# Block products in one more token group, with the forms of w4 on VectorE

## The chip, the cores and the metric

One core of one Trainium2 chip runs the kernel. The metric is the device time of one execution in microseconds (us). PE is the matrix engine, DVE the vector engine, ACT the scalar engine, POOL the GpSimd engine, SP the engine whose queue issues the DMAs.

## The reference

With x of 2048 tokens by 448 channels, `_layernorm` without gain and the tanh form of gelu:

```python
def _A_ref(x, w_r, w_i):              # spectral filter
    X = rfft2(x, axes=(-2, -1))
    X = X * (w_r + 1j * w_i)
    return irfft2(X, s=(S, D), axes=(-2, -1))
def _B_ref(x, w1, w2, w3, w4):        # shifted token mixing, then an MLP of width 1792
    h = _gelu(_layernorm(x) @ w1)
    hs = shifted(h) @ w2              # four quarters of the channels, tokens shifted by +1, -1, +2, -2
    x1 = x + hs
    h2 = _gelu(_layernorm(x1) @ w3) @ w4
    return x1 + h2
xn = _layernorm(x)
return x + _A_ref(xn, A_w_r, A_w_i) + _B_ref(xn, B_w1, B_w2, B_w3, B_w4)
```

All inputs and the output are fp32.

## The kernel before

fp32 operands are split into two fp16 numbers, a high and a low half (`hi`, `lo`), and a product is made as hi x hi + hi x lo + lo x hi, three passes on PE.

**The MLP.** The 2048 tokens are eight groups G of 256 (two blocks of 128), the 1792 hidden channels seven pairs fp of 2 x 128. One unit (G, fp) is a `front` and a `back`. `front` multiplies w3 by the tokens (22 matmuls of 256 columns into one PSUM bank), then ACT applies gelu and writes the high half of h (`hf`, L776), and DVE writes the low half (L777). `back` multiplies h by w4 into the two accumulators `acc` of the group, over all seven fp: 12 matmuls of 448 columns for two token blocks, two channel tiles and three passes.

In the groups named in `STR` (5, 6 and 7 before), the two cross passes hi x lo and lo x hi, 8 of the 12 matmuls, are made another way (`crossed`): the 2 x 2 blocks (token block by channel tile, channel tile by column half) are multiplied with seven products in place of eight, as in Strassen's scheme. Each product is a matmul of 224 columns for either pass, 14 in all; hi x hi stays as 4 matmuls of 448 columns. This needs sums and differences ("forms") of h, made by `forms` on DVE into `hgm` (three operations per unit, L786 to L788), forms of w4, made once by `w4_forms` into `w4x` (its lines L928 to L932), and two more PSUM accumulators `cr` from the banks with the tag "tr". At the end of such a group, `back` copies `cr` out by ACT into `cross` (L843), makes four additions there (L846), evacuates `acc` by DVE (L835), and adds `cross` to the result (L850). `cross` is the memory of `x2mem` from fp32 element 4F on, where w4's raw rows 12 and 13 lay before, and where later the second buffer of the spectral chunks (`pf_buf[1]`) lies.

`steps` writes out the order of the units: the front of unit n+2 goes ahead of the back of unit n (`ahead=AH`), the forms of unit n+1 too. `run` emits them with a late priority (`FILL`); evacuations and forms have the first (`EVAC`). `tags` names the PSUM banks of the fronts: two "mm" banks, or "mm" and "tr" in turn, four banks.

**The spectral part** runs between the units. Folds: for each pair of token blocks, `do_fold` loads x into one of four fold buffers, normalizes it on ACT and adds and subtracts mirrored columns on POOL; `step1_in` splits it (L594 on ACT, L595 on DVE) into `xh`; `step1` multiplies (L604) and splits the result (L608, L609). Then 16 chunks (`chunk_a`, `chunk_b`, `chunk_z`, `chunk_c`) in groups 3 and 4, then 16 inverse steps. `w_scale` loads the filter in eight pieces and takes their maxima on DVE (L269), `w_scale_end` makes a power of two from them with a transpose (L627) and a broadcast (L631) on PE. `ln2` normalizes token blocks for the MLP (L549, L551 on DVE).

**What sets the order.** The program builder orders instructions by priority and a model of their times, and the order is then fixed for each engine. `behind(key)` holds an instruction until the one filed under the key is issued: ("f", G, fp) is the end of a front's evacuation, ("m", G, fp) the last matmul of a back, ("X", b) the load of a fold, ("fold", b) its last addition. The lists `FOLD` (when a fold starts), `PACE` (after which back its matmuls come), `WMAX` (when each maximum is taken) and `LATE` (the normalization of blocks 12 to 15) hold such keys.

Of the kernel before, what the change touches and what calls it, by code (L numbers as in the profile page):

```python
# [12 lines left out]
F32 = mybir.dt.float32  # L13
F16 = mybir.dt.float16
# [17 lines left out]
AH = 2  # L32
PACE = [(0, 6), (1, 1), (1, 2), (1, 4), (1, 5), (2, 0), (2, 1), (2, 3)]
FOLD = [(0, 5), (1, 0), (1, 1), (1, 3), (1, 4), (1, 6), (2, 0), (2, 2)]
PIN = [("a3",), ("a3",), ("a3",), ("a3",)]
WMAX = [(1, 4), (1, 5), (2, 0), (2, 0), (2, 1), (2, 2), (2, 3), (2, 4)]
LATE = [(2, 2), (2, 3), (2, 4), (2, 5)]
HS = 3
STR = (5, 6, 7)
INV, LAG = 4, 2  # L40
EVAC, FILL = 0, 100000

# [80 lines left out]
def body(tc, nc, x, wf, w1, w2, w3, w4, c_g, c_n, c_small, out):  # L123
# [59 lines left out]
    warm = pc.tile([128, 1], F32, name="warm")  # L183
    V.memset(warm, 0.0)
    A.activation(out=warm, in_=warm, func=AF.Gelu_apprx_tanh)
    x2mem = pw.tile([128, 9 * F], F16, name="x2mem")
    wsrc = x2mem[:, 8 * F:8 * F + 512]
    V.memset(wsrc, 0.0)
    ones = pc.tile([128, 128], F32, name="ones")
# [33 lines left out]
    load_w3([2, 3])  # L223
    cross = x2mem.bitcast(F32)[:, 4 * F:4 * F + 2 * D].rearrange("p (i n) -> p i n", i=2)
    x2all = x2mem[:, 0:8 * F].rearrange("p (j t n) -> p j t n", j=4, t=7)
    w4raw = x2mem.bitcast(F32)[:, F:].rearrange("p (f n) -> p f n", f=14)
    W4F = (0, 4, 8, 11, 14)
    w4x = pw.tile([128, 48 * 224], F16, name="w4x")
    hgm = pw.tile([128, 2, 1024], F16, name="hgm")
# [339 lines left out]
    folds = {}  # L569

    def do_fold(b0):
        f = xf_buf[b0 // 2 % 4]
        X = f.rearrange("p b s d -> p (b s d)")[:, 0:2 * D + 2].rearrange("p (b d) -> p b d", b=2)
        after["X", b0] = (SY.dma_start(X[:, :, 0:D], xv[:, b0:b0 + 2]).ins,)
        with behind("f", *FOLD[b0 // 2]):
            for i in range(2):
                x_ = X[:, i, 0:D]
                A.activation(out=x_, in_=x_, func=AF.Identity, scale=xn_scale[b0 + i], bias=xn_bias[b0 + i])
            A.activation(out=X[:, :, D:D + 1], in_=X[:, :, 0:1], func=AF.Copy)  # L579
        ad = X[:, :, 0:D].rearrange("p b (h d) -> p h b d", h=2)[:, :, :, 0:113]  # L580
        bc = X[:, :, 1:D + 1].rearrange("p b (h d) -> p h b d", h=2)[:, ::-1, :, 223:110:-1]
        u = xr.rearrange("p (a b s d) -> p a b s d", a=2, b=2, s=2)
        P.tensor_tensor(out=u[:, 0], in0=ad, in1=bc, op=ALU.add)  # L583
        P.tensor_tensor(out=u[:, 1], in0=ad, in1=bc, op=ALU.subtract)
        for k, op in ((0, ALU.add), (2, ALU.subtract)):
            i = P.tensor_tensor(out=f[:, :, k:k + 2].rearrange("p b s d -> p s b d"), in0=u[:, :, 0], in1=u[:, :, 1], op=op)
        after["fold", b0] = (i.ins,)
        for i in range(2):
            folds[b0 + i] = f[:, i].rearrange("p s d -> p (s d)")
# [201 lines left out]
    def back(G, fp):  # L791
        h = hs.pop((G, fp))
        n = D // 2
        end = 4 if G == 7 else 6
        if fp == 0:
            acc[G] = [bank("acc", f"acc{G}{i}") for i in range(2)]
            if G in STR:
                xs[G] = [bank("tr", f"cr{G}{i}") for i in range(2)]
        if (G, fp) == (7, 5):
            xs[G] = [bank("tr", f"end{i}") for i in range(2)]  # L800
        C = [[(slice(0, D), acc[G][i][:, 0:D], 0, 6)] for i in range(2)]
        if G == 7:
            C[1] = [(slice(0, D), acc[G][1][:, 0:D], 0, 4)]
            if fp > 4:
                C[1] = [(slice(n * k, n * k + n), xs[G][k][:, 0:n], 5, 6) for k in range(2)]
        for i in range(2):
            for r, to, s, e in C[i]:
                with behind("m", G, fp) if (G, fp) == (7, 6) and ("m", G, fp) in after else contextlib.nullcontext():
                    for f in range(2):
                        for hi, wi in ((0, 0),) if crossed(G, fp) else ((0, 0), (0, 1), (1, 0)):  # L810
                            m = T.matmul(to, h[:, hi, 2 * f + i], w4p[0][:, wi, 2 * fp + f, r],  # L811
                                         start=fp == s and f == 0 and hi + wi == 0, stop=fp == e and f == 1 and hi == 1)
                after["m", G, fp] = (m.ins,)
            if not i and not crossed(G, fp):
                yield keep(m)
        if crossed(G, fp):
            g = hg.pop((G, fp))
            X = [xs[G][k // 2][:, n * (k % 2):n * (k % 2) + n] for k in range(4)]
            H = [[acc[G][i][:, n * k:n * k + n] for k in range(2)] for i in range(2)]
            prods = [(0, 1, X[0], 9), (1, 3, H[1][0], 9), (3, 2, H[0][0], C[0][0][3]), (6, 4, X[2], 9),  # L820
                     (4, 5, X[3], end), (5, 6, X[1], end), (2, 7, H[1][1], C[1][0][3])]
            for hi, wi, part in ((0, 1, 0), (1, 0, 0), (0, 1, 1), (1, 0, 1)):
                if hi + part == 1 and wi == part:
                    yield keep(m)
                for k, slot, to, e in prods[3 * part:3 + 4 * part]:
                    m = T.matmul(to, h[:, hi, slot] if slot < 4 else g[:, hi, slot - 4], w4f[fp][k][wi], start=k in (0, 6) and fp == 0 and hi == 0,  # L826
                                 stop=hi == 1 and fp == e)
            after["m", G, fp] = (m.ins,)
        k34 = p34[:, 1:2] if G >= 6 else p34[:, 0:1]
        to = {i: rest[2 * G + i] if G >= 6 else xb(2 * G + i) for i in range(2)} if fp >= 4 else {}  # L830

        def evacuate(i):
            for r, src, _, e in C[i]:
                if fp == e:
                    V.scalar_tensor_tensor(out=to[i][:, r], in0=src, scalar=k34, in1=to[i][:, r], op0=ALU.mult, op1=ALU.add)  # L835
                    if G == 7 and fp == 6:
                        SY.dma_start(ov[:, 2 * G + i, r], to[i][:, r])

        with prio(EVAC):
            if G in STR and fp == end:  # L840
                e0, e1 = cross[:, 0], cross[:, 1]
                for i in range(2):
                    A.activation(out=cross[:, i], in_=xs[G][i][:, 0:D], func=AF.Copy, scale=k34)  # L843
                for o, x, y in ((e0[:, n:], e0[:, 0:n], e0[:, n:]), (e1[:, 0:n], e1[:, 0:n], e0[:, n:]),
                                (e0[:, n:], e0[:, n:], e1[:, n:]), (e1[:, n:], e1[:, 0:n], e1[:, n:])):
                    (V if G == 7 else P).tensor_tensor(out=o, in0=x, in1=y, op=ALU.add)  # L846
            for i in range(2):
                evacuate(i)
                if G in STR and fp == end:
                    (V if G == 7 else P).tensor_tensor(out=to[i], in0=to[i], in1=cross[:, 1 - i], op=ALU.add)  # L850
                if G == 6 and fp == 6:
                    SY.dma_start(ov[:, 2 * G + i], to[i])
        yield keep(m)
# [27 lines left out]
    def mlp(*args, **kw):  # L881
        run(steps(*args, **kw))
# [38 lines left out]
    def w4_forms(fp):  # L921
# [1 line left out]
        b = [[w4p[0][:, :, f + r, n * c:n * c + n] for c in range(2)] for r in range(2)]  # L923
        m = w4all[:, 56 * 224:] if fp == 6 else w4x[:, 8 * 224 * fp:8 * 224 * (fp + 1)]
        m = m.rearrange("p (k n) -> p k n", n=224)
        t1 = [m[:, 6], m[:, 7]]
        t2, t3, t4 = (m[:, k:k + 4:3] for k in range(3))
        P.tensor_tensor(out=t3, in0=b[1][1], in1=b[0][1], op=ALU.add)  # L928
        for i in range(2):
            P.tensor_tensor(out=t1[i], in0=b[0][0][:, i], in1=b[0][1][:, i], op=ALU.subtract)  # L930
            P.tensor_tensor(out=t2[:, i], in0=b[1][1][:, i], in1=t1[i], op=ALU.subtract)
        P.tensor_tensor(out=t4, in0=b[1][0], in1=t2, op=ALU.subtract)  # L932
        w4f[fp] = [[x[:, i] for i in range(2)] for x in (b[0][0], b[1][0], b[1][1], t4)]
        w4f[fp] += [t1] + [[x[:, i] for i in range(2)] for x in (t2, t3)]

    def squares1():
        for t in range(4):
# [165 lines left out]
    Y1 = Y.rearrange("p i q c (b k) -> p i q c b k", k=8)  # L1103
    pfd = pool("pfd", side="right")
    xf_buf = [pfd.tile([128, 2, 4, 113], F32, name=f"xf{i}") for i in range(3)]
    xf_buf.append(hgm.bitcast(F32).rearrange("p i n -> p (i n)")[:, 0:904].rearrange("p (b s d) -> p b s d", b=2, s=4))
    xh_buf = [pfd.tile([128, 2 * 452 + 16], F16, name=f"xh{i}") for i in range(4)]
    for i in range(4):
        P.memset(xh_buf[i][:, 904:], 0.0)
    mlp([1, 2], ahead=AH, tags=("mm", "tr"))  # L1110
    for b in range(0, NB, 2):
        do_fold(b)
        step1_in(b)
        step1_in(b + 1)
        with behind("m", *PACE[b // 2]):
            step1(b)
            step1(b + 1)
    with prio(FILL):
        for fp in range(7):
            with behind("fold", 0 if fp < 2 else 14):  # L1120
                w4_forms(fp)
    ln2(range(12, 16), [A] * 4, LATE)
    with behind("X", 14):
        wm = w_scale()
    close("pfd")
    with behind("m", 2, 5):
        w_scale_end(wm)
    pst = pool("pst", side="right")
    pf_buf = [pst.tile([128, 2, 2, DF], F16, name="pf0"),
# [68 lines left out]
```

## Time and profile before

| | |
|---|---|
| median of 3 runs | 410.64 us (409.51 to 411.13) |
| profiled execution | 409.72 us, its span 407.6 us |
| PE, DVE, ACT, POOL busy | 98%, 75%, 66%, 44% of the span |
| tensor clock granted | 0.999 |

"Busy" is the share of the span in which an engine had an instruction under way. The chain is the sequence of work that ended last, followed back from the last instruction. In listings of groups, the first number behind the bar is busy us, the next the mean ns of one instruction, then idle time before it and what ended it. In a row of waits stand the total in us, the number of times and the longest one. In the timeline and the chain the first number is the start in us from the start of the span, the second the length in us.

### The profile page before, as it was taken

Reading aid. Unit: us, or ns where it says so; the run is one execution under the profiler, and the core shown is the slowest. Engines: PE = TensorE matmul, PEld = TensorE weight load, DVE = VectorE, ACT = ScalarE, POOL = GpSimd, SP = SyncE. Lnnn points to the kernel's source line nnn. Section 1 sums busy time; section 2 is a strip of 40 time slices with the busy share of each in tenths; the row PEclk is TensorE's granted clock in tenths of the full one; section 3 lists DMA queues with packets and bytes.
Section 4 is the critical chain, followed back from the end, with each engine's and each line's share of the span. In section 5 each row is a group of like instructions: output and inputs, shape, how many; then the busy total and the mean of one; then the engine's idle time right before and its main releaser. Section 6 shows DMA issues by size and latency. Waiting matters only on the chain.

```text
span 407.6 us, 8828 instructions
## 1 busy us (share of the span) xinstructions
PE 401.3 (98%) x3379; PEld 296.0 (73%) x3379; DVE 304.2 (75%) x658; ACT 268.6 (66%) x465; POOL 179.8 (44%) x276
## 2 busy tenths in 40 slices
PE   8998999999999999999999999999999999999996
PEld 4553555666767777776888887877788888888885
DVE  5988999899653757894577777763488879889645
ACT  4698993884737865763488888785956566544332
POOL 3889723011197747499243344441231254217100
PEclk9999999999999999999999999999999999999999
DMA  8999999915910375317055666642000022323201
GB/s 282 351 274 198 177 180 261 260 23 109 207 48 0 92 233 175 103 36 170 19 135 146 151 145 151 153 112 60 2 2 2 24 68 75 108 70 112 92 2 45
DMA packets 57209, 49.46 MB, mean 121 GB/s; under 512 B 41312, under 2 KB 52192, under 8 KB 57168
## 3 DMA queue, kind: packets, MB, share of 16 engines
q1 hardware_dynamic: 57168, 48.91, 46.4%
q8 instruction: 26, 0.43, 0.5%
q14 instruction: 15, 0.12, 0.1%
HBM read 35.06 MB, written 3.67 MB: 95 GB/s over the span
## 4 chain that ended last, share of the span: by engine, by line
PE 96%; DMA 2%; ACT 1%; DVE 0%; issue 0%; ACTq 0%
PE pw L435 33%; PE acc L811 24%; PE pw L510 9%; PE pw L465 6%; PE cr L826 4%; PE acc L826 3%; PE pu L707 3%; PE ps L604 3%; PE pp L661 2%; PE pe L727 2%; PE px L678 2%; PE py L749 2%; PE wps L889 2%; DMA h<-hs 2%; PE pta L414 1%; PE end L811 1%
## 5 line engine op out<-in xcount | busy, mean ns | idle before, releaser
L435 PE MATMUL pw<-x2mem,w3p 128*128 128x256 f16 x1232 | 149.7, 272 | 0.0
L435 PEld LDWEIGHTS <-w3p 128*128 128x128 f16 x1232 | 118.7, 98 | 19.4
L811 PE MATMUL acc<-w4p,hf 128*128 128x448 f16 x508 | 107.4, 352 | 0.0
L811 PEld LDWEIGHTS <-hf 128*128 128x128 f16 x532 | 51.5, 98 | 35.5
L777 DVE SCALAR_TENSOR_TENSOR hf<-pw,h,hf 128x512 f16<-128x512 f32 x56 | 41.8, 747 | 36.5 <-ACT hf L776 36.3
L773 ACT ACTIVATE pw<-pw,pe 128x512 f32<-128x512 f32 x56 | 36.7, 656 | 44.8 <-PE pw L435 44.6
L510 PE MATMUL pw<-w2p,h 112*128 112x448 f16 x192 | 39.2, 353 | 1.3 <-DMA h<-hs 1.2
L734 POOL TENSOR_TENSOR e<-e 128x226 f32<-128x226 f32 x16 | 11.1, 696 | 63.7 <-ACT e L731 56.2
L776 ACT ACTIVATE hf<-pw,h 128x512 f16<-128x512 f32 x56 | 38.3, 683 | 1.3
L465 PE MATMUL pw<-w1p,w4x 128*128 128x448 f16 x176 | 34.8, 352 | 0.5 <-DVE h L967 0.5
L510 PEld LDWEIGHTS <-h 112*128 112x128 f16 x192 | 18.4, 98 | 18.0 <-DMA h<-hs 2.2
L688 POOL TENSOR_TENSOR xr<-te 128x450 f32<-128x450 f32 x16 | 15.7, 981 | 34.5 <-DVE te L686 34.5
L465 PEld LDWEIGHTS <-w4x 128*128 128x128 f16 x176 | 17.1, 98 | 16.4 <-ACT w4x L424 0.7
L696 POOL TENSOR_TENSOR zb<-xr,zb 128x450 f16<-128x450 f32 x16 | 16.1, 1009 | 16.8 <-ACT zb L695 16.8
L684 DVE SCALAR_TENSOR_TENSOR te<-px,sc,wc 128x450 f32<-128x450 f32 x16 | 11.0, 685 | 10.6 <-ACT te L683 7.0
L683 ACT ACTIVATE te<-px 64x450 f32<-64x450 f32 x32 | 17.2, 538 | 1.7 <-PE px L678 1.2
L719 ACT ACTIVATE U<-y 113x512 f16<-113x512 f16 x32 | 18.0, 620 | 0.1
L741 ACT ACTIVATE vh<-e 128x448 f16<-128x448 f32 x16 | 9.2, 575 | 13.5 <-DVE e L739 13.3
L731 ACT ACTIVATE e<-pe 128x452 f32<-128x452 f32 x16 | 8.7, 545 | 14.0 <-PE pe L727 11.6
L540 POOL TENSOR_SCALAR y<-xt,nm 128x448 f32<-128x448 f32 x6 | 5.9, 986 | 23.3 <-DMA x2mem<-y 12.9
L711 DVE SCALAR_TENSOR_TENSOR y<-pu,y 113x512 f16<-113x512 f32 x16 | 10.9, 687 | 6.9 <-ACT y L710 6.8
L583 POOL TENSOR_TENSOR xr<-xf 128x452 f32<-128x452 f32 x6 | 6.7, 1125 | 20.6 <-ACT xf L579 10.5
(208 smaller groups left out, 799.0 us busy)
## 6 DMA issues: line engine op xcount, KB each, us to landing
wc<-wf SPq DMA_DIRECT2D x32, 225.0 KB, 3.8
wl<-wf SPq DMA_DIRECT2D x8, 450.0 KB, 3.9
xt<-x SPq DMA_DIRECT2D x3, 896.0 KB, 11.3
w3raw<-w SPq DMA_DIRECT2D x3, 896.0 KB, 14.6
xf<-x SPq DMA_DIRECT2D x6, 448.0 KB, 3.7
xr<-x SPq DMA_DIRECT2D x12, 224.0 KB, 2.5
out<-xr SPq DMA_DIRECT2D x12, 224.0 KB, 2.0
gn<-c_g SPq DMA_DIRECT2D x16, 128.0 KB, 3.2
```

The costliest lines, as they stand in the source:

```text
L435: m = T.matmul(ps_out, wp[:, wi + t, cols], xT[:, xi + t, tok], start=t == 0 and wi + xi == 0, stop=t == 3 and wi == 4)
L465: m = T.matmul(pm[:, :D], xTs[g][:, xi + t, 128 * i:128 * i + 128], w1p[:, wi + t], start=t == 0 and p == 0, stop=t == 3 and p == 2)
L510: m = T.matmul(w2b[b][:, :D], hT[g][:112, 4 * hi + k, o:o + 128], w2p[:, wi, k], start=k == 2 and hi + wi == 0, stop=k == 3 and hi == 1)
L683: i = A.activation(out=e[64 * h:64 * h + 64], in_=px_[64 - 64 * h:128 - 64 * h, :2 * DF], func=AF.Copy)
L688: P.tensor_tensor(out=z, in0=t[:, 0], in1=t[:, 1], op=ALU.add)
L696: P.tensor_tensor(out=zv[1], in0=z, in1=zv[0], op=ALU.subtract)
L719: A.activation(out=U[b][:113, p].rearrange("p q (c k) -> p q c k", c=NC), in_=Y1[:113, p, :, :, b], func=AF.Copy)
L773: A.activation(out=pm, in_=pm, func=AF.Gelu_apprx_tanh, scale=r3)
L776: i = A.activation(out=h[:, 0], in_=pv_, func=AF.Copy, scale=h3)
L777: j = V.scalar_tensor_tensor(out=h[:, 1], in0=pv_, scalar=h3, in1=h[:, 0], op0=ALU.mult, op1=ALU.subtract)
L811: m = T.matmul(to, h[:, hi, 2 * f + i], w4p[0][:, wi, 2 * fp + f, r], start=fp == s and f == 0 and hi + wi == 0, stop=fp == e and f == 1 a ...
L826: m = T.matmul(to, h[:, hi, slot] if slot < 4 else g[:, hi, slot - 4], w4f[fp][k][wi], start=k in (0, 6) and fp == 0 and hi == 0, stop=hi ...
```

## The change

Group 2, the third, is put into `STR`. What goes with it:

- The fronts of group 2 use the "mm" banks only, since `cr` takes the "tr" banks.
- All of w4's forms are made before group 2, on DVE in four operations per pair instead of six on POOL: four pairs behind front (0,6), three behind fronts (1,0) to (1,2).
- `hgm` is needed for group 2, so the fourth fold buffer, which lay in it, moves into `x2mem` where `cross` lies. The eight folds use the buffers in the order of `FBUF`: the fourth buffer once, and the last fold takes the first one.
- The units of groups 1 and 2 are emitted step by step, with the folds between them, instead of all ahead of the folds.
- The keys of the maxima (`WMAX`) and of `w_scale_end` are later ones.
- At the end of group 6 the additions of `cross` are on DVE as in group 7; those of groups 2 and 5 are on POOL.

```diff
+FBUF = (0, 1, 2, 3, 0, 1, 2, 0)
-WMAX = [(1, 4), (1, 5), (2, 0), (2, 0), (2, 1), (2, 2), (2, 3), (2, 4)]
+WMAX = [(1, 5), (1, 6), (2, 1), (2, 2), (2, 3), (2, 4), (2, 5), (2, 5)]
-STR = (5, 6, 7)
+STR = (2, 5, 6, 7)
...
-    x2mem = pw.tile([128, 9 * F], F16, name="x2mem")
+    x2mem = pw.tile([128, 9 * F + 16], F16, name="x2mem")
...
-        f = xf_buf[b0 // 2 % 4]
+        f = xf_buf[FBUF[b0 // 2]]
...
-                    (V if G == 7 else P).tensor_tensor(out=o, in0=x, in1=y, op=ALU.add)
+                    (V if G > 5 else P).tensor_tensor(out=o, in0=x, in1=y, op=ALU.add)
...
-                    (V if G == 7 else P).tensor_tensor(out=to[i], in0=to[i], in1=cross[:, 1 - i], op=ALU.add)
+                    (V if G > 5 else P).tensor_tensor(out=to[i], in0=to[i], in1=cross[:, 1 - i], op=ALU.add)
...
-        t1 = [m[:, 6], m[:, 7]]
+        t1 = m[:, 6:8]
         t2, t3, t4 = (m[:, k:k + 4:3] for k in range(3))
-        P.tensor_tensor(out=t3, in0=b[1][1], in1=b[0][1], op=ALU.add)
-        for i in range(2):
-            P.tensor_tensor(out=t1[i], in0=b[0][0][:, i], in1=b[0][1][:, i], op=ALU.subtract)
-            P.tensor_tensor(out=t2[:, i], in0=b[1][1][:, i], in1=t1[i], op=ALU.subtract)
-        P.tensor_tensor(out=t4, in0=b[1][0], in1=t2, op=ALU.subtract)
+        for o, x, y, op in ((t3, b[1][1], b[0][1], ALU.add), (t1, b[0][0], b[0][1], ALU.subtract),
+                            (t2, b[1][1], t1, ALU.subtract), (t4, b[1][0], t2, ALU.subtract)):
+            V.tensor_tensor(out=o, in0=x, in1=y, op=op)
...
-    xf_buf.append(hgm.bitcast(F32).rearrange("p i n -> p (i n)")[:, 0:904].rearrange("p (b s d) -> p b s d", b=2, s=4))
+    xf_buf.append(x2mem.bitcast(F32)[:, 4 * F:4 * F + 904].rearrange("p (b s d) -> p b s d", b=2, s=4))
...
-    mlp([1, 2], ahead=AH, tags=("mm", "tr"))
+    gen = steps(range(1, 3), ahead=AH, tags=["mm", "tr"] * 3 + ["mm"] * 8)
+    with prio(FILL):
+        for fp in range(4):
+            with behind("f", 0, 6):
+                w4_forms(fp)
+    while ("f", 1, 3) not in after:
+        run(gen, len(slots))
+        n = len(w4f)
+        if n < 7 and ("f", 1, n - 4) in after:
+            with prio(FILL), behind("f", 1, n - 4):
+                w4_forms(n)
     for b in range(0, NB, 2):
+        while ("m", *PACE[b // 2]) not in after:
+            run(gen, len(slots))
         do_fold(b)
...
-    with prio(FILL):
-        for fp in range(7):
-            with behind("fold", 0 if fp < 2 else 14):
-                w4_forms(fp)
+    run(gen)
     ln2(range(12, 16), [A] * 4, LATE)
...
-    with behind("m", 2, 5):
+    with behind("m", 2, 6):
         w_scale_end(wm)
```

More of the change, by code (lines that the diff above doesn't have):

```diff
@@ L225, in body @@
     x2all = x2mem[:, 0:8 * F].rearrange("p (j t n) -> p j t n", j=4, t=7)
-    w4raw = x2mem.bitcast(F32)[:, F:].rearrange("p (f n) -> p f n", f=14)
+    w4raw = x2mem.bitcast(F32)[:, F:9 * F // 2].rearrange("p (f n) -> p f n", f=14)
     W4F = (0, 4, 8, 11, 14)
@@ L925, in w4_forms @@
         m = m.rearrange("p (k n) -> p k n", n=224)
-        t1 = [m[:, 6], m[:, 7]]
+        t1 = m[:, 6:8]
         t2, t3, t4 = (m[:, k:k + 4:3] for k in range(3))
-        P.tensor_tensor(out=t3, in0=b[1][1], in1=b[0][1], op=ALU.add)
-        for i in range(2):
-            P.tensor_tensor(out=t1[i], in0=b[0][0][:, i], in1=b[0][1][:, i], op=ALU.subtract)
-            P.tensor_tensor(out=t2[:, i], in0=b[1][1][:, i], in1=t1[i], op=ALU.subtract)
-        P.tensor_tensor(out=t4, in0=b[1][0], in1=t2, op=ALU.subtract)
+        for o, x, y, op in ((t3, b[1][1], b[0][1], ALU.add), (t1, b[0][0], b[0][1], ALU.subtract),
+                            (t2, b[1][1], t1, ALU.subtract), (t4, b[1][0], t2, ALU.subtract)):
+            V.tensor_tensor(out=o, in0=x, in1=y, op=op)
         w4f[fp] = [[x[:, i] for i in range(2)] for x in (b[0][0], b[1][0], b[1][1], t4)]
-        w4f[fp] += [t1] + [[x[:, i] for i in range(2)] for x in (t2, t3)]
+        w4f[fp] += [[x[:, i] for i in range(2)] for x in (t1, t2, t3)]
     def squares1():
```

## The prediction

> **What bounds the kernel now.** I read the page first (busy shares, then the chain that ended last), then PE's own waits, then busy time by stage, then single instructions of the stages that the edit touches.
>
> ```profile
> span 407.6 us, 8828 instructions
> ...
> PE 401.3 (98%) x3379; PEld 296.0 (73%) x3379; DVE 304.2 (75%) x658; ACT 268.6 (66%) x465; POOL 179.8 (44%) x276
> ...
> PE 96%; DMA 2%; ACT 1%; DVE 0%; issue 0%; ACTq 0%
> ```
>
> PE is busy for 401.3 of 407.6 us and makes up 96% of the chain. A busy PE could still hide short gaps, so next come the waits of PE, all that there are:
>
> ```profile
> PE wps L889 <- DVE x2mem L188: 1.2, 1, 1.2
> PE pw L510 <- DMA h<-hs: 1.2, 1, 1.2
> PE pw L465 <- DVE h L967: 0.5, 1, 0.5
> ```
>
> All three lie in the first 40 us, in the warm-up and the w1/w2 part. From there on PE waits for nothing until its last matmul. So a matmul taken out between 150 and 200 us is time won, as long as no wait appears; and there is no old wait in the middle which the edit could remove as a bonus. The gain is capped by the matmul time saved; the loss is not capped.
>
> Busy time by stage (columns: length, then busy us and instructions of PE, PEld, DVE, ACT, POOL, the clock, DMA share, GB/s). The first row is most of token group 2 as it is now, the second a stretch of group 5, which already has the block products:
>
> ```profile
> 160.00:194.00 34.00, 34.00 (x283) 24.48 (x282) 26.21 (x37) 19.86 (x33) 28.19 (x37) 1.00 0.46 116
> 305.00:331.60 26.60, 26.60 (x260) 22.18 (x258) 22.57 (x53) 15.57 (x29) 7.37 (x11) 1.00 0.10 32
> ```
>
> PE fills both to the end. DVE stands at 77% in the first and 85% (22.57 of 26.60) in the second, still without one PE wait. ACT, at 58%, gets only two copies more, at the very end of group 2. DVE is the engine to watch.
>
> **Part 1, the products: minus 1.26 us.** Rows of the chain (start, length), one unit of group 2 as it is, then one of group 7 with products between its neighbours:
>
> ```profile
> 171.44 2.27 PE acc L811 x12
> 383.90 2.40 PE pw L435 x22
> 386.31 0.76 PE acc L811 x4
> 388.40 2.40 PE pw L435 x22
> ```
>
> A plain unit is 12 matmuls of 448 columns, 2.27 us. A unit with products is 4 of these plus 14 of 224 columns, and it runs from 386.31 to 388.40: 2.09 us, of which the 14 take 1.33, 95 ns each. The difference is 0.18 us, and group 2 has seven units: 7 x 0.18 = 1.26 us. Six more instructions per unit each bring a weight load:
>
> ```profile
> L826 PEld LDWEIGHTS <-hgm x152: 97/98/98, 301.3 to 397.0; 128*128 128x128 f16 x152
> ```
>
> A load is shown at 98 ns and the spacing at 95, so loads and matmuls overlap almost exactly; were the 14 bound by loads of 98 ns end to end, a unit would take 0.76 + 1.37 = 2.13 us and the seven would save 0.98. I take the measured spacing, which contains whatever the loads do. The Trainium skill, "TensorE: Matmul & The Clock Gate", section "LDWEIGHTS (loading the stationary operand)", gives a load columns / 1.2 ns, 107 ns for 128; if that paced the 14, an estimate from it would be 0.76 + 1.49 = 2.25 us per unit and only 0.14 us saved in all. The trace differs: 98 ns for the load, 95 from start to start.
>
> **Part 2, the forms of h: 21 more DVE operations.** Each unit of group 2 now needs three DVE subtractions before its products. Of those there are rows, from groups 5 to 7 (min/median/max ns):
>
> ```profile
> L786 DVE TENSOR_TENSOR hgm<-hf x19: 409/426/949, 291.7 to 393.0; 128x512 f16<-128x512 f16 x19
> L788 DVE TENSOR_TENSOR hgm<-hf,hgm x19: 274/291/674, 292.5 to 393.8; 128x256 f16<-128x256 f16 x19
> ```
>
> L787 has the same shape as L788. So 0.426 + 2 x 0.291 = 1.01 us per unit, 7.06 for the seven. They lie beside PE: between the end of a front and its back stand two other fronts and two backs, 2 x (2.40 + 2.09) = 9.0 us. At nothing, then, while DVE keeps up.
>
> **Part 3, w4's forms from POOL to DVE.** Four DVE operations of 448 half-precision elements for each of seven pairs, 28 in all. No row has this shape; between the 256 and 512 elements above lies 0.291 + 0.75 x 0.135 = 0.39 us, 10.9 us in sum, with 28 x 0.291 = 8.1 and 28 x 0.426 = 11.9 as ends. They are asked for behind fronts (0,6) to (1,2), that is from about 104 us on:
>
> ```profile
> 104.00:157.00 53.00, 53.00 (x444) 39.19 (x443) 29.52 (x43) 35.29 (x63) 35.06 (x36) 1.00 0.43 113
> ```
>
> DVE has 53.00 - 29.52 = 23.5 us free there, twice the need, and the first product needs them only in group 2. Cost nothing. What they leave behind on POOL matters more. Four of its groups between 160 and 194 us, and the DVE operations of the same stretch:
>
> ```profile
> L930 POOL TENSOR_TENSOR w4x<-w4p 128x224 f16<-128x224 f16 x8 | 5.8, 739 | 0.0
> L931 POOL TENSOR_TENSOR w4x<-w4p,w4x 128x224 f16<-128x224 f16 x8 | 4.9, 640 | 0.0
> L928 POOL TENSOR_TENSOR w4x<-w4p 128x448 f16<-128x448 f16 x4 | 4.4, 1110 | 0.0
> L932 POOL TENSOR_TENSOR w4x<-w4p,w4x 128x448 f16<-128x448 f16 x3 | 3.0, 1024 | 0.0
> ```
> ```profile
> L551 DVE SCALAR_TENSOR_TENSOR y<-y,vs 128x384 f16<-128x384 f32 x4 | 4.4, 1088 | 0.0
> L269 DVE TENSOR_REDUCE wm<-wl 128x1 f32<-128x900 f32 x4 | 4.3, 1077 | 0.0
> L595 DVE TENSOR_TENSOR xh<-xf,xh 128x452 f16<-128x452 f32 x4 | 3.9, 1006 | 0.0
> L549 DVE SCALAR_TENSOR_TENSOR y<-y,vs 128x64 f16<-128x64 f32 x4 | 2.6, 642 | 1.3 <-ACT y L548 1.3
> L595 DVE TENSOR_TENSOR xh<-hgm,xh 128x452 f16<-128x452 f32 x2 | 2.4, 1243 | 0.0
> ```
>
> Over the whole run the same DVE lines are far shorter at their median or minimum:
>
> ```profile
> L549 DVE SCALAR_TENSOR_TENSOR y<-y,vs x16: 268/279/889, 48.3 to 184.8; 128x64 f16<-128x64 f32 x16
> L551 DVE SCALAR_TENSOR_TENSOR y<-y,vs x16: 603/612/1429, 48.5 to 185.4; 128x384 f16<-128x384 f32 x16
> L595 DVE TENSOR_TENSOR xh<-xf,xh x12: 611/1011/1487, 115.1 to 166.1; 128x452 f16<-128x452 f32 x12
> ```
>
> So while POOL is at work, DVE operations that read two SBUF tensors stretch: 4 x (1.088 - 0.612) + 4 x (0.642 - 0.279) + 4 x (1.006 - 0.611) + 2 x (1.243 - 0.611) = 6.2 us in this stretch. The four POOL groups are 18.1 of POOL's 28.19 us, 64%, and they go: I credit DVE with 0.64 x 6.2 = 4.0 us.
>
> **Part 4, the last fold's buffer and the maxima of the filter.** The last fold now takes buffer 0, which the fold of blocks 8 and 9 holds until its low half is written; before, it went into hgm's memory.
>
> ```profile
> 142.51 0.37 SPq L574 DMA_DIRECT2D hgm<-x  x1
> 149.86 0.62 DVE L595 TENSOR_TENSOR xh<-xf,xh 128x452 f16<-128x452 f32 x1
> 166.88 0.75 DVE L777 SCALAR_TENSOR_TENSOR hf<-pw,h,hf 128x512 f16<-128x512 f32 x1 [0.19 <-ACT hf L776]
> 107.44 1.14 DVE L292 SCALAR_TENSOR_TENSOR w4p<-x2mem,pe,w4p 128x896 f16<-128x896 f32 x1
> ```
>
> Its load moves from 142.5 to after 150.5 us, and the eight filter loads, held behind it on SP's queue, move with it, about 8 us. Nobody is short of them: the fold is wanted behind front (2,2), whose low half is written from 166.9 us on (third row), and the maxima are given later keys. Two maxima move past 160 us: 2 x 1.077 = 2.15 us more DVE in that stretch. The other new buffer, in w4's raw rows, must wait for the last split of w4, done at 108.6 us (fourth row), and belongs to the fourth fold, behind front (1,3), which runs after 127 us with the other fronts of group 1: nothing.
>
> **The sum on DVE between 160 and 194 us:** 26.21 + 7.06 + 2.15 - 4.0 = 31.4 us, against a PE time that shrinks to 34.0 - 1.26 = 32.7. That is 96%, above the 85% that group 5 carries without a wait, but under one. This is the thin place of the forecast.
>
> **Part 5, the hand-over from group 2 to 3.** Group 2 now ends as group 5 does: two ACT copies, four POOL additions, two evacuations on DVE, two more POOL additions, in memory whose first half is the second pf buffer of the spectral chunks. Group 5's last matmul ends where the first row starts; its last POOL pair is the second row. The third row is the first write into that pf buffer.
>
> ```profile
> 331.45 1.47 PE L435 MATMUL pw<-x2mem,w3p 128*128 128x256 f16 x12
> 336.36 2.40 POOL L850 TENSOR_TENSOR xt<-xt,x2mem 128x448 f32<-128x448 f32 x2
> 200.35 0.53 ACT L668 ACTIVATE x2mem<-pp 64x450 f16<-64x450 f32 x1
> ```
> ```profile
> 195.38 0.87 PE pw L435 x8
> 196.25 0.31 PE wpb L631 x2
> ```
>
> The tail lasts 338.76 - 331.45 = 7.3 us. The pf write now comes 200.35 - 195.38 = 5.0 us after group 2's end, so chunk 1 is put off by about 2.3 us; the ACT instruction that waits holds the next gelu behind it. Cover: three fronts of group 3, 3 x 2.40 = 7.2 us of matmuls that need none of it, after them backs and chunk 0. The scaling of the filter (one transpose, one broadcast on PE, DVE steps between) moves from behind unit (2,5) to behind (2,6), under the same fronts. Bounds: 0, or all 2.3 us exposed; I take 0.3, near zero, because the 195.38 handover itself shows no PE wait today.
>
> Group 6's additions move from POOL to DVE, and group 6 already has DVE room as in the 85% row; nothing.
>
> **Total.** The profiled execution took 409.72 us, 2.1 around its span; the three others took 409.51, 410.64 and 411.13. The four average 410.25. Minus 1.26, plus 0.3: 409.3 us. In the span of a run like the profiled one that is 407.6 - 1.0 = 406.6. The median given for before, 410.64, lies a little above the mean, so the step against it may read as 1.3 rather than 1.0.
>
> **Rivals.**
> (a) DVE becomes the bound of group 2, and the kernel gets slower. Price: no relief from POOL (its folds stay), half of the forms stretched by 1.78 as L551 is (1.088 / 0.612): 26.21 + 9.8 + 2.15 = 38.2 us, 5.4 over PE's 32.7; 410.25 - 1.26 + 5.4 = 414.4. With no relief alone it is 35.4, 2.7 over, 411.7. It decides once DVE's work passes 32.7 us. For it: the stretched rows above, and an order that is fixed when the program is built. Against: POOL's 18.1 us do go, and PE can run some 5 us ahead of DVE before it feels it. The Trainium skill, "SBUF — State Buffer", section "Who interferes with whom", has a DVE instruction with two SBUF inputs and a GpSimd one that reads SBUF exclude each other, the later one waiting in full. The stretched rows fit that; it would bear on all 49 operations put on DVE.
> (b) The pf buffer's wait comes through: 410.25 - 1.26 + 2.3 = 411.3.
> (c) The products are bound by weight loads: 0.98 saved, 409.6 with the 0.3. This is how the change could fall short of what it says; against it stand groups 5 to 7, measured.
>
> **How the numbers follow.** About 0.5%, 2.05 us, is what a measurement of this kernel tells from no change. Chances: forecast 0.68, (a) 0.14, (b) 0.14, (c) 0.04. Faster by over 0.5% means below 408.6, which takes the saving and a lucky median, given that single runs spread over 1.6 us: a sixth of forecast and (c), 0.12. Slower means above 412.7: most of (a), 0.12. The rest, 0.76, is same. Range: down to 408.2, the lowest run shown less the saving (409.51 - 1.26), and up to 411.9, just past (b) and the mild form of (a).
>
> **What would show it.** Right: group 2's backs at 2.09 us in the chain; no PE wait between 100 and 300 us; DVE near 31 us in the 34 after 160; L549 and L551 back near 0.28 and 0.61 us; the span about one us shorter. Wrong: PE waits on hf, hgm or xh from DVE (a), or near 200 us on pp and px (b); backs at 2.13 us or more (c).

## The result, and the profile after

The changed kernel takes 413.69 us (median of 11 runs, 411.01 to 416.85) against 410.44 us for the one before, run on the same chip (11 runs, 408.44 to 412.22): 1.0092 times as long, with a 95% interval of 1.0068 to 1.0116. It is about 0.9% slower. The forecast was 409.3 us, in a range of 408.2 to 411.9.

The profiled execution is the slowest of the eleven, 416.85 us; its stalls may be larger than those of a median run, and its times aren't to be set against the medians. From its page (span, busy times, shares of the chain that ended last):

```profile
span 414.8 us, 8950 instructions
...
PE 402.6 (97%) x3421; PEld 300.6 (72%) x3421; DVE 319.1 (77%) x713; ACT 269.1 (65%) x467; POOL 145.6 (35%) x234
...
PE 79%; DVE 10%; DMA 3%; issue 2%; ACT 1%; POOL 1%; SPq 0%; DVEq 0%; POOLq 0%
```

The span grew by 7.2 us. PE's idle time went from 6.3 to 12.2 us (span less busy), which is 5.9 of it; its busy time grew by 1.3 us although seven units are shorter. DVE, which had no visible part in the old chain, now makes up 10% of it, and DMA 3%. All waits of PE, in us (total, times, longest):

```profile
PE ps L605 <- DVE xh L596: 3.5, 2, 2.9
PE ps L605 <- DVE y L610: 1.5, 2, 1.0
PE wps L890 <- DVE x2mem L189: 1.2, 1, 1.2
PE acc L812 <- DVE xt L836: 1.2, 2, 0.8
PE pw L466 <- DVE h L966: 0.5, 1, 0.5
PE pw L511 <- DMA h<-hs: 0.4, 1, 0.4
PE cr L827 <- DVE hf L778: 0.3, 1, 0.3
PE pta L415 <- POOL xt L361: 0.2, 1, 0.2
```

Three names are new and large enough to matter: xh, y and xt, all from DVE. By stage they fall into two places (same columns as in the prediction: length, busy us of PE, PEld, DVE, ACT, POOL, clock, DMA share, GB/s):

```profile
119.00:160.00 41.00, 37.47 (x326) 28.65 (x324) 27.66 (x39) 25.11 (x46) 20.30 (x19) 0.96 0.26 86
160.00:194.00 34.00, 31.33 (x310) 26.05 (x309) 29.67 (x49) 22.03 (x40) 9.91 (x12) 1.00 0.48 108
```

PE loses 3.53 us in the first stretch, the wait on xh, and 2.67 us in the second, the waits on y and xt. In neither is DVE full over the whole stretch: 27.66 of 41.00 us and 29.67 of 34.00. So a sum over the stretch doesn't show either stall. A narrower window does show something for the second: all its waits lie between 170 and 181 us, and there DVE works almost without a pause, 22.00 of 23.00 us:

```profile
161.00:184.00 23.00, 20.33 (x198) 16.43 (x196) 22.00 (x34) 15.05 (x28) 8.75 (x9) 1.00 0.36 97
```

**The first stall, at 137 us.** From the chain (start, length) and from the timeline:

```profile
126.45 2.19 DVE w4x L931 x2
128.66 1.07 DVE w4x L931
...
131.55 1.61 DVE w4p L931 x2
133.19 1.07 DVE w4p L931
...
135.47 2.83 DVE xh L596 x2
138.34 0.98 PE ps L605 x10
139.33 3.37 PE pw L436 x18
```
```profile
129.51 1.05 ACT L595 ACTIVATE xh<-xf 128x452 f16<-128x452 f32 x2 [1.28 <-POOL xf L587]
129.56 1.09 POOL L584 TENSOR_TENSOR xr<-xf 128x452 f32<-128x452 f32 x1
...
130.61 1.21 POOL L585 TENSOR_TENSOR xr<-xf 128x452 f32<-128x452 f32 x1
...
131.48 4.07 DVE L931 TENSOR_TENSOR w4p<-w4p 128x448 f16<-128x448 f16 x4
131.89 2.11 POOL L587 TENSOR_TENSOR xf<-xr 128x452 f32<-128x452 f32 x2
...
137.01 0.73 PE L605 MATMUL ps<-csm,xh 128*128 128x128 f16 x10 [2.93 <-DVE xh L596]
```

ACT had written its part of xh by 130.56 us, but DVE's part of it began at 135.47, 4.9 us later: the last forms of w4 (L931) stand before it in DVE's fixed order. Four of them take 4.07 us there, about 1.02 each in the mean. POOL is running its fold additions at the same time, 1.05 to 1.2 us each: about one DVE operation gets through for each POOL operation. The same instructions beside an idle POOL take 0.38 us (min/median/max ns, first and last start):

```profile
L931 DVE TENSOR_TENSOR w4x<-w4p x12: 380/382/1174, 113.2 to 127.5; 128x448 f16<-128x448 f16 x12
L931 DVE TENSOR_TENSOR w4p<-w4p x4: 586/1114/1266, 131.5 to 134.3; 128x448 f16<-128x448 f16 x4
```

PE then pays twice. It waits 3.5 us, and afterwards its clock is halved (the eighth figure is the granted clock):

```profile
137.00:138.00 1.00, 0.73 (x10) 0.56 (x10) 1.00 (x1) 0.22 (x1) 0.92 (x2) 1.00 0.00 0
138.00:139.00 1.00, 0.66 (x9) 0.66 (x10) 1.00 (x3) 0.38 (x1) 1.00 (x1) 0.83 0.00 0
139.00:140.00 1.00, 1.00 (x9) 0.76 (x7) 1.00 (x2) 0.60 (x1) 0.13 (x1) 0.50 0.51 59
140.00:141.00 1.00, 1.00 (x6) 0.74 (x5) 1.00 (x3) 0.00 (x0) 0.00 (x0) 0.50 0.92 337
141.00:142.00 1.00, 1.00 (x7) 0.71 (x5) 0.35 (x1) 0.00 (x0) 0.00 (x0) 0.50 0.78 129
142.00:143.00 1.00, 1.00 (x9) 0.72 (x8) 0.00 (x0) 0.26 (x1) 0.00 (x0) 0.96 0.85 263
```

Summed over these rows, 0.17 + 3 x 0.50 + 0.04, 1.7 us of clock are lost, and the 18 matmuls of 3.37 us are spaced 187 ns apart where 22 of the kind take 2.40 us, 109 each. In this execution the stall costs about 3.5 + 1.7 = 5.2 us. The clock's part seems not to be in every run: 1.7 of 414.8 us make a mean clock of 0.996, and eight of the eleven runs have 0.995 or 0.996 (414.7 us in their mean), while three have 0.999 or 1.0 (412.2).

**The second stall, after 158 us.** From the timeline, the filter's loads and the maxima that read them:

```profile
153.38 0.37 SPq L575 DMA_DIRECT2D xf<-x  x1
153.84 0.89 SPq L619 DMA_DIRECT2D wl<-wf  x2
...
161.72 2.22 DVE L270 TENSOR_REDUCE wm<-wl 128x1 f32<-128x900 f32 x2 [3.82 <-DMA wl<-wf]
```

The last fold's load moved from 142.51 to 153.38 us and the filter loads went with it, 11 us. Not all of that is the new buffer's doing: in after_xh_only below, which has the same buffer and no first stall, this load goes out at 150.04, 7.5 us later than before. The first filter load is also slow: it lands 8.5 us after its issue, against a median of 3.3 for the eight. The fold's load, a second filter load and four loads of x are issued within 4 us of it; that they slow it is not shown by a run. From the chain:

```profile
154.31 8.52 DMA wl<-wf
```

DVE, in its fixed order, sits 3.8 us before the first maximum, while the subtractions of h, the hf and the y that PE needs stand behind it. All eight maxima then start in the 34 us after 160, beside the new forms of h, and DVE works on almost without a pause until 184 us. PE's 2.7 us of waits on y and xt follow. So the late maximum starts this stall, and DVE's full load behind it passes it on to PE.

### The profile page after: what moved, and what is told of

Its sections match the earlier page's. It is cut to its first block, busy times and chain, and to the rows that moved or that the text cites. A ratio compares the mean times of both kernels' runs of the same rounds, so it can differ in the third digit from the quotient of the medians.

```text
span 414.8 us, 8950 instructions
## 1 busy us (share of the span) xinstructions
PE 402.6 (97%) x3421; PEld 300.6 (72%) x3421; DVE 319.1 (77%) x713; ACT 269.1 (65%) x467; POOL 145.6 (35%) x234
## 4 chain that ended last, share of the span: by engine, by line
PE 79%; DVE 10%; DMA 3%; issue 2%; ACT 1%; POOL 1%; SPq 0%; DVEq 0%; POOLq 0%
PE pw L436 27%; PE acc L812 17%; PE pw L511 9%; PE pw L466 6%; PE cr L827 4%; PE acc L827 3%; PE pu L708 3%; PE pp L662 2%; PE px L679 2%; PE pe L728 2%; DMA wl<-wf 2%; PE py L750 2%; DVE hf L778 1%; PE ps L605 1%; DMA h<-hs 1%
## 5 line engine op out<-in xcount | busy, mean ns | idle before, releaser
L436 PE MATMUL pw<-x2mem,w3p 128*128 128x256 f16 x1232 | 152.2, 274 | 0.0
L436 PEld LDWEIGHTS <-w3p 128*128 128x128 f16 x1232 | 119.9, 98 | 19.9
L812 PE MATMUL acc<-w4p,hf 128*128 128x448 f16 x452 | 97.6, 352 | 1.2 <-DVE xt L836 1.2
L812 PEld LDWEIGHTS <-hf 128*128 128x128 f16 x476 | 45.9, 98 | 31.1 <-issue 1.5
L778 DVE SCALAR_TENSOR_TENSOR hf<-pw,h,hf 128x512 f16<-128x512 f32 x56 | 41.8, 746 | 31.7 <-ACT hf L777 29.2
L584 POOL TENSOR_TENSOR xr<-xf 128x452 f32<-128x452 f32 x7 | 7.8, 1120 | 43.1 <-issue 34.8
L827 PEld LDWEIGHTS <-hgm 128*128 128x128 f16 x208 | 20.0, 98 | 0.0
L827 PE MATMUL cr<-w4x,hgm 128*128 128x224 f16 x138 | 19.4, 259 | 0.0
L827 PEld LDWEIGHTS <-hf 128*128 128x128 f16 x156 | 14.8, 98 | 5.0 <-DVE hf L778 0.5
```

The source lines that it names most:

```text
L436: m = T.matmul(ps_out, wp[:, wi + t, cols], xT[:, xi + t, tok], start=t == 0 and wi + xi == 0, stop=t == 3 and wi == 4)
L778: j = V.scalar_tensor_tensor(out=h[:, 1], in0=pv_, scalar=h3, in1=h[:, 0], op0=ALU.mult, op1=ALU.subtract)
```

## The experiments

Each line is the median of the runs, in us, and the ratio to before on the same chip with its 95% interval. The theory going in was that both stalls are matters of order on DVE (forms ahead of xh; late filter loads), not of the amount of work; the rival was the prediction's rival (a), too much work on DVE in group 2.

| kernel | median | ratio |
|---|---|---|
| the change | 413.69 | 1.0092 [1.0068, 1.0116] |
| forms_pool | 417.64 | 1.0193 [1.0149, 1.0238] |
| wl_early | 412.57 | 1.0056 [1.0035, 1.0077] |
| both | 415.85 | 1.0140 [1.0111, 1.0169] |
| no_products | 413.52 | 1.0079 [1.0053, 1.0106] |
| fbuf3 | 412.43 | 1.0044 [1.0023, 1.0064] |
| before_fbuf0 | 409.93 | 0.9996 [0.9975, 1.0018] |
| after_xh_only | 410.94 | 1.0012 [0.9990, 1.0035] |
| after_xh | 407.96 | 0.9937 [0.9917, 0.9958] |
| forms_small | 407.60 | 0.9916 [0.9889, 0.9943] |
| xh_no_products | 408.73 | 0.9949 [0.9929, 0.9968] |
| xh_pair_products | 407.76 | 0.9950 [0.9932, 0.9968] |
| xh_pair_plain | 408.74 | 0.9975 [0.9963, 0.9986] |

**forms_pool: w4's forms back on POOL, at the new place in the program.**

```diff
-            V.tensor_tensor(out=o, in0=x, in1=y, op=op)
+            P.tensor_tensor(out=o, in0=x, in1=y, op=op)
```

> The changed kernel with w4's forms made by the same four operations per pair, at the same keys, but on POOL instead of DVE. Theory 1 (w4's forms on DVE): 12 of them stand in DVE's fixed order before the low halves xh of the second fold, and stretch from 0.38 to about 1.1 us while POOL adds the folds; PE waits 3.5 us on xh near 137 us and then runs some 2 us at a slower clock. It expects no PE wait on xh between 120 and 145 us, DVE's median work there some 10 us less, and a time about 4 to 5 us below the changed kernel's median of 413.7, so 408.7 to 409.7. Theory 2 (the filter loads come late, DVE waits in order 3.8 us for the first of them near 158 us): it expects that this run still shows that wait and the PE waits after it, and a gain of under 2 us. Theory 3 (too much DVE work in group 2, forms of h and eight maxima, whatever the rest): little gain, above 412.

It came out slowest of all, 417.64 us. The wait on xh is gone, but a larger one stands elsewhere (PE's waits, then the timeline):

```profile
PE acc L812 <- DVE hf L778: 5.7, 1, 5.7
```
```profile
105.00 2.02 POOL L931 TENSOR_TENSOR w4x<-w4p 128x448 f16<-128x448 f16 x2
105.09 0.97 DVE L302 TENSOR_SCALAR nib<-nib 128x4 int32<-128x4 int32 x1
...
106.09 0.94 DVE L304 TENSOR_TENSOR nqb<-nib 128x4 f32<-128x4 f32 x1
...
107.07 0.96 DVE L305 TENSOR_TENSOR nqb<-nqb,vb 128x4 f32<-128x4 f32 x1
```

POOL ran the forms from 88.5 us on, for `behind()` orders the instructions when the program is built and holds nothing back on an engine that has nothing else to do. DVE's small operations of layer norm, four columns each, then took 0.94 to 0.97 us, one for each POOL operation of 1.01 us; L302 has a median of 0.17 us over its five instances. The hf behind them came 5.7 us late. The 408.7 to 409.7 us expected for theory 1 were missed by far, and the time lies where theory 3 had it, above 412, though by this wait and not by work in group 2. The run is thus no clean test of where the forms belong: it swaps one stall of the same kind for a larger one.

**wl_early: the filter's loads and maxima earlier in the order.**

```diff
-    with behind("X", 14):
+    with behind("X", 10):
         wm = w_scale()
```

> The changed kernel with the loads of the filter behind the sixth fold's load instead of the eighth's; the orders of PE, ACT and POOL stay the same, on DVE two maxima move a few places ahead. Theory 2 (late filter loads): DVE's wait of 3.8 us for the first filter load goes, with it the PE waits of 2.7 us on acc, hf and y between 167 and 182 us; the wait on xh near 137 us stays; time 2 to 3.5 us below the changed kernel, 410.2 to 411.7. Theory 1 (w4's forms): the waits after 160 us come from DVE being late already; gain under 1 us. Theory 3 (too much DVE work in group 2): the waits between 167 and 182 us stay, without a DMA behind them, gain under 1 us.

The second stall goes entirely, the first stays as it was:

```profile
160.00:194.00 34.00, 34.00 (x339) 28.86 (x338) 29.32 (x56) 22.94 (x41) 9.81 (x12) 1.00 0.48 103
```
```profile
PE ps L605 <- DVE xh L596: 3.5, 2, 2.9
```

PE is busy for all 34.00 us while DVE does 29.32 of work, hardly less than the 29.67 with which the change lost 2.67. So in group 2 the amount of DVE's work alone stalls nothing; it takes the late maximum ahead of it. This speaks against rival (a) as it was worded. The gain in the medians, 1.1 us, is less than the 2 to 3.5 expected, and the two intervals overlap a little.

**both: the two edits together.** The diffs are the two above.

> The changed kernel with both edits, w4's forms on POOL and the filter loads behind the sixth fold's load. If theories 1 and 2 each hold for one of the two stalls, both go, PE waits for nothing between 100 and 300 us, and the time is that of before less the saving in matmuls: 410.4 - 1.3 = 409.1, between 408.6 and 409.8. Theory 3 (too much DVE work in group 2): PE waits remain after 160 us and the time stays at or above that of before.

415.85 us, with the wait on hf at 6.2 us, where 408.6 to 409.8 were expected: the 1.8 us between it and forms_pool are the loads' part, and the forms on POOL keep their own stall.

**no_products: the rest of the change without the block products in group 2.**

```diff
-STR = (2, 5, 6, 7)
+STR = (5, 6, 7)
```

> The changed kernel with group 2 out of the list of groups with products: w4's forms still early and on DVE, the buffers, filter loads and keys as changed, but no products, no forms of h and no second accumulators in group 2. Leaves out only the products, so PE has 1.26 us more of matmuls. Theories 1 and 2: the wait on xh near 137 us and DVE's wait for the filter load near 158 us stay, the time is 412.5 to 415. Theory 3 (the forms of h make DVE the bound): no PE waits after 160 us, time near that of before, 410 to 411.5.

413.52 us, not to be told from the change. The wait on xh is there (2.9 us); in the 34 us after 160 PE loses nothing, with DVE at 25.43. DVE waits only 1.6 us for the filter there. What the products save and what the forms of h bring into the second stall seem about equal, and most of the loss needs no products at all. after_xh below shows that it comes from the place of w4's forms on DVE.

**fbuf3 and before_fbuf0: the fold buffer alone.** The first undoes the last fold's buffer in the change, the second does it alone in the kernel before.

```diff
-FBUF = (0, 1, 2, 3, 0, 1, 2, 0)
+FBUF = (0, 1, 2, 3, 0, 1, 2, 3)
```
```diff
-        f = xf_buf[b0 // 2 % 4]
+        f = xf_buf[(0, 1, 2, 3, 0, 1, 2, 0)[b0 // 2]]
```

> The changed kernel with the last fold in the fourth buffer, as before, instead of the first; PE's order is the same. Theory 2, in the form that the last fold's buffer is what holds the filter loads back: the load of the last fold and the filter loads go out some 6 us earlier, DVE's wait near 158 us goes as it did in the run with early filter loads, and the time is that run's, 411.5 to 413.0. If the buffer is not the cause: DVE's wait stays and the time is 413 to 414.

> The kernel before with only the last fold's buffer changed to the first one; PE's order is that of before. Theory 2: the filter loads go out some 8 us later, DVE waits in order for the first of them near 155 us, 2 to 5 us, but with DVE's load in group 2 as low as before (77%) PE waits for at most 1 us: 410 to 411. If the late loads cost by themselves, whatever DVE's load: 412 to 414.

fbuf3 takes 412.43 us, like wl_early: the second stall is gone by another way, the first is left. before_fbuf0 takes 409.93, no change. DVE's and PE's waits of before_fbuf0:

```profile
DVE wm L269 <- DMA wl<-wf: 3.8, 2, 2.0
```
```profile
PE acc L811 <- DVE xt L835: 0.2, 1, 0.2
```

The late loads make DVE wait 3.8 us there too, and PE feels 0.2 of it. In no_products they cost PE nothing either. In these runs they cost time only where DVE has the forms of h to do besides.

**after_xh_only and after_xh: the last three pairs of forms behind the xh of a fold.** The second has wl_early's edit as well.

```diff
-        n = len(w4f)
-        if n < 7 and ("f", 1, n - 4) in after:
-            with prio(FILL), behind("f", 1, n - 4):
-                w4_forms(n)
 ...
         step1_in(b + 1)
+        if b in (2, 4, 6):
+            with prio(FILL), behind("x", b + 1):
+                w4_forms(len(w4f))
```

> The changed kernel with the last three pairs of w4's forms behind the xh of folds two to four, the filter loads as late as in the change. Theory 1: the wait on xh near 137 us goes, and 3.5 to 5 us with it. Theory 2 (late filter loads): DVE's wait on the filter load near 158 us stays with 1 to 4 us of PE waits after it, different from run to run; median 409 to 411, spread over 3 us or more.

> The run with early filter loads, and the last three pairs of w4's forms on DVE behind the low halves of folds two, three and four instead of behind fronts (1,0) to (1,2), so that in DVE's order they stand behind the xh that PE waited for. Theory 1 (w4's forms in front of xh, each stretched by an addition on POOL): the wait of 3.5 us on xh and the slower clock after it go; PE waits for nothing over 0.5 us between 100 and 300 us; time 410.0 - 1.3 = 408.7, between 408.2 and 409.7. Theory 3 (DVE has too much work in groups 1 and 2, wherever it stands): the wait moves to another matmul and the time stays near 412.

after_xh_only takes 410.94 us, as long as before, and keeps the second stall (group 2's stage):

```profile
160.00:194.00 34.00, 30.65 (x296) 25.55 (x294) 31.70 (x59) 19.30 (x33) 7.26 (x9) 1.00 0.55 127
```

after_xh takes 407.96, faster than both kernels: 0.6% less than before, and a little below the 408.2 to 409.7 expected. PE's largest waits in after_xh, and its stages:

```profile
PE wps L890 <- DVE x2mem L189: 1.2, 1, 1.2
PE pw L466 <- DVE h L966: 0.5, 1, 0.5
PE ps L605 <- DVE y L610: 0.4, 1, 0.4
```
```profile
119.00:160.00 41.00, 40.64 (x372) 31.55 (x370) 32.63 (x47) 29.55 (x55) 23.50 (x22) 1.00 0.32 108
160.00:194.00 34.00, 34.00 (x333) 29.20 (x332) 28.37 (x55) 19.83 (x35) 7.41 (x10) 1.00 0.59 126
```

The same 28 forms on the same engine, DVE busier in the first stretch (32.63 against 27.66 us), and both stalls are gone. Nor did the forms become short: the last twelve take 8.4 us here, 10.1 in wl_early, and five of them still 1.1 us each beside POOL. So it was their place in the order that made the first stall, and the place of the late maximum that set off the second. In time: 412.57 - 407.96 = 4.6 us for the place of the forms with early loads, near the 5.2 read from the trace, and 413.69 - 410.94 = 2.8 with late ones; 410.94 - 407.96 = 3.0 us for the late loads once the first stall is away, against 1.1 (413.69 - 412.57) while it is there. Only the 3.0 is known to compare runs of one chip. The two don't add up as separate prices. The runs also lie closer together: 407.62 to 408.82 over 12 runs.

**forms_small: is it the length of the forms?** On wl_early, the twelve operations of the last three pairs work on 32 of 224 columns; the products of these pairs use the fourth pair's forms.

```diff
+            k = 224 if fp < 4 else 32
-            V.tensor_tensor(out=o, in0=x, in1=y, op=op)
+            V.tensor_tensor(out=o[:, :, 0:k], in0=x[:, :, 0:k], in1=y[:, :, 0:k], op=op)
```

> The run with early filter loads and the last three pairs' 12 operations still in front of xh, but each cut to 32 of 224 columns, 64 elements in place of 448; nobody reads them, the products of those pairs use the fourth pair's forms. The number and place of the operations stays, their size falls to a seventh. If each DVE operation waits for the POOL addition under way, whatever its own size: those near an addition still take 0.7 to 1.1 us, and PE still waits 1.5 to 3.5 us on xh near 137 us. If they stretch in proportion to their size: 0.2 to 0.35 us each, and the wait on xh goes, as does the slower clock after it; time 408.5 to 409.7.

Mixed. A seventh of the elements doesn't make a seventh of the time beside POOL:

```profile
L932 DVE TENSOR_TENSOR w4p<-w4p x4: 193/712/1096, 129.5 to 131.3; 128x64 f16<-128x64 f16 x4
```

It takes 0.19 us alone, 0.71 in the median and up to 1.1 us beside POOL: the length is mostly POOL's, not the operation's own. But the last eight took 5.7 us instead of 8.6, xh began at 132.08 instead of 135.25, and that was enough: 407.60 us, below the 408.5 expected at the least, with PE's wait on xh gone. For operations that wait for POOL whatever their size, 1.5 to 3.5 us of that wait were expected to stay. PE feels nothing until the delay has used up its lead, so 3.2 us of delay less took away all 3.5 us of waits and the slow clock after them.

**xh_no_products, xh_pair_products and xh_pair_plain: what the products are worth.** after_xh without the products in group 2; then both once more, on one chip. The edit is no_products' own.

> The version with early filter loads and w4's forms behind xh, with group 2 out of the list of groups with products; leaves out only the products and their forms of h. If the 1.26 us of matmuls are worth their time where PE waits for nothing: 407.96 + 1.26 = 409.2, between 408.8 and 409.7, and below before's 410.1 by what the earlier forms and filter loads bring. If the products win nothing or the version gains from something else: 407.6 to 408.3.

> The kernel with the last three pairs of w4's forms behind xh and the early w_scale, the products in group 2 kept, once more beside its twin without them on the same chip. If the products are worth the 1.26 us of the prediction's part 1: this one 1.26 us below the twin, the two intervals against before apart by about 0.3%. If the first two series' difference (about 0.5 to 0.9 us from different calls) is right: 0.1 to 0.2% apart. If DVE's 21 extra operations eat what PE saves: no difference.

> The twin without the products in group 2 (four shifted passes there, all else the same). If the products are worth 1.26 us: ratio to before about 0.997, 1.26 us above the other. If they are worth 0.5 to 0.9 us: 0.995 to 0.996. If nothing: the same ratio as the other.

On one chip 407.76 us with the products (407.53 to 408.51) and 408.74 without (408.18 to 409.44): 0.98 us, the ratios 0.25% apart, with intervals that overlap by 0.05%. With products the kernel does 42 more matmuls in less time, and PE is busy for 34.00 of 34.00 us either way. xh_no_products takes 408.73 us, 0.8 above after_xh, but on another chip.

## Why the prediction was wrong, by its own steps

**Part 1, the products: right.** A back takes 2.10 us in the chain of the change (185.07 to 187.17), 2.09 predicted:

```profile
185.07 0.76 PE acc L812 x4
187.17 2.40 PE pw L436 x22
```

Measured on the whole, 0.98 of 1.26 us. That is also what the load-bound form, rival (c), gave; the two readings are 0.28 us apart, and the intervals don't tell them from each other. The back of 2.10 us does: rival (c) wanted 2.13 or more.

**Part 2, the forms of h at nothing: right by themselves.** In after_xh, which has them, PE loses nothing between 160 and 194 us. Their length was right only away from POOL: in the change the fifteen between 160 and 194 us take 8.4 us, where 5 x 1.01 = 5.1 were predicted, and the first three, beside fold additions, 0.95 to 1.03 each.

**Part 3, w4's forms on DVE: this is the step that failed.** The duration was right where POOL is idle (0.38 us, 0.39 predicted). "DVE has 23.5 us free there, twice the need [...] Cost nothing" was wrong, in two ways. The duration was not asked for at the time where the instructions stand: the last eight run beside the fold additions and take 8.6 us, 1.07 each in the mean. The prediction itself had read that stretch off the stretched rows and applied it to group 2 only. And free time was added up over 53 us, while the order of one engine is a line: the forms stood in front of xh, and xh had 4.9 us to wait. That is a price of 4.6 us by the runs (2.8 with late loads), where the forecast had 0. Placing them behind xh makes "cost nothing" true.

**The relief from POOL: right for the operations it was read from.** Between 160 and 194 us the operations on y are back at their own length:

```profile
L552 DVE SCALAR_TENSOR_TENSOR y<-y,vs 128x384 f16<-128x384 f32 x3 | 1.8, 609 | 0.0
...
L550 DVE SCALAR_TENSOR_TENSOR y<-y,vs 128x64 f16<-128x64 f32 x3 | 0.8, 277 | 2.0 <-ACT y L549 2.0
```

**Part 4, "Nobody is short of them": the second step that failed.** The mechanism was seen, the filter loads did move with the fold (11 us, 8 predicted; 7.5 without the first stall). Eight maxima came to start past 160 us, though, where six were reckoned with. What was missed is who is queued behind the instruction that waits for them: a maximum with a later key still has its fixed place on DVE, and it held the forms of h, hf and y. Its price was 1.1 to 3.0 us by the runs. The sum on DVE, 31.4 us predicted, came out at 29.67; over the whole stretch it decided nothing, but behind the late maximum DVE had no time left to catch up (22.00 of 23.00 us).

**Part 5, the hand-over: right at nothing.** No PE wait near 200 us on pp or px; rival (b) is out. After 194 us PE waits only once, 0.3 us on hf between 385 and 395 us. Group 6's additions on DVE, forecast at nothing, may have caused it, but no_products has them too and not this wait.

**Rival (a)** names the right engine and gave 411.7 to 414.4, which holds the 413.69; but that is luck: its mechanism, work over 32.7 us, is not what happened, and at 29.67 us its own condition was not met. DVE did bound group 2 from 161 to 184 us, but only behind the late maximum, and the larger stall came before group 2's products. Its chance of 0.14 was too small because the argument against it, PE's lead of some 5 us, was set against a mean load instead of against the longest stretch that could stand before one needed instruction.

What the Trainium skill says in "SBUF — State Buffer", section "Who interferes with whom", that of a DVE instruction with two SBUF inputs and a GpSimd one that reads SBUF the later waits in full, fits the stretched forms of w4 (0.38 us to 1.07 in the mean, beside POOL operations of 1.05 to 1.2). The prediction had said that it would bear on all 49 operations put on DVE, and its sum then charged none of these eight.

**Left open.** xh_pair_plain, which has no products, is still 0.25% faster than before (0.9975 [0.9963, 0.9986]); the relief of DVE from POOL's work is a candidate, but no run isolates it, and the profiled run of before also has a wait of 1.2 us on the load of h in its first 40 us (0.4 in before_fbuf0, none in xh_pair_plain) which the change doesn't touch. Nor did I find why the runs of the change spread over 5.8 us; the slower clock, in eight of the eleven, goes with some 2.5 us of it (414.7 against 412.2).

## What to carry to other kernels

Before moving work to an engine with free time, look up which instruction will stand in front of which in its fixed order, and take the duration from the time at which it will run, with what the neighbouring engine does then. A load that comes later is dear not through its reader but through all that is queued behind the reader. Work that nobody needs soon goes behind the instruction that the bounding engine is waiting for, not in front of it.

## What was not expected of the hardware

- Beside a stream of POOL operations a DVE operation with two SBUF inputs can last about as long as one POOL operation, however small it is: 448 elements 1.02 to 1.07 us in the mean (0.38 alone), 64 elements up to 1.10 (0.19 alone, 0.71 in the median of four), four columns 0.94 and 0.96 (L304, with 0.14 in its median, and L305). In proportion small operations lose most. The four-column L302 has one input, and was stretched too (0.97, with 0.17 in its median). L778, one of whose inputs lies in PSUM, was not: 0.72 to 0.75 us in all 56 cases of forms_pool.
- A PE that had done nothing for 2.93 us was granted half its clock about 1.7 us after it had started again (137.01 us; the 0.83 of the slice from 138 puts the drop near 138.7), for 3.4 us (to near 142.1): 1.7 us lost on top of the wait. The Trainium skill, "TensorE: Matmul & The Clock Gate", section "Part 1: The HAM clock gate (the "warmup" mystery)", gives an activity window of 3413 ns after which an idle PE is throttled and a busy one released. The length of the slow stretch agrees with it; the gap before it, 2.93 us, was shorter than that window.
